# A gated mix of windowed attention and a GEGLU block: q weights and chunk 0's rows loaded another way, a few evictions and the last product changed

## The chip, the core and the metric

The kernel runs on one core of a Trainium2 chip. The core has TensorE (PE, matrix products; weight loads are listed as PEld), VectorE (DVE), ScalarE (ACT), GpSimd (POOL), SyncE (SP, which issues most DMAs), and 16 DMA engines. The metric is device time in microseconds (us) from start to end of one execution; a time of a kernel is the median of several executions. The profile is that of one execution.

## The reference

The input x has 2048 rows of 1024 columns, in bf16. Two blocks are applied to it and mixed row by row:

```python
g = sigmoid((x * gate_w).sum(-1, keepdims=True))
# block A: 32 heads of 32 columns; a row sees itself and 7 rows before it, 2 apart
q, k, v = split(x @ wqkv)                     # wqkv: 1024 x 3072
logits = q . k[pos - 2*w] / sqrt(32)          # w = 0..7, masked where pos - 2*w < 0
a = (softmax(logits) weighted sum of v[pos - 2*w]) @ wo
# block B: gate and up 1024 x 3584, down 3584 x 1024
b = (gelu(x @ w_gate) * (x @ w_up)) @ w_down
out = g * a + (1 - g) * b
```

## The kernel before, in words

**Tiling.** The rows form four chunks of 512, taken in two pairs (a pair is a "sup"). Each large product is done on 2 x 2 blocks with seven products in place of eight (Strassen-Winograd), so sums of weight blocks and of input blocks are needed. TensorE works on 128x128 weight tiles and 512 columns at a time; an accumulator is one of eight PSUM banks. Weights pass through `ring`, 20 slots of 256 KB. The columns of x (or of the weights' rows) come in eight tiles, kt = 0..7, halves of four.

**Stages.** For pair 0: q (`first_pair`), k, v projections (`qkv_pair`), then gate/up (`ffn`, 28 column tiles), then `down` for chunk 0. For pair 1: down and projections in the order q, v, k, and so on; `down(3)` is last, with seven products m for each of two row groups g. The attention of a chunk, with scores (L937, L943) and weighted sums (L1084 to L1102), is VectorE's work beside TensorE's products.

**What sets the order.** A planner, `Weave`, runs while the program is built. Each stream of work is a generator of operations with an estimated cost and dependencies. At every step the planner emits the head of the stream with the smallest start time plus bias. A stream's bias is dropped when the operation's `due` time is nearer than `AHEAD`. What it emits on one engine stays in that order on the chip. `main()` alone holds TensorE's operations, so their order is that of the text; the planner mixes VectorE's and the DMA issues.

**The start.** Chunk 0's rows, first half of their columns, come by two DMAs (L312): rows 0 to 255 from SyncE, 256 to 511 from ScalarE. `turn_rows` (L541 on) turns them on TensorE, four 128x128 transposes for each of four row tiles j; VectorE and ScalarE empty the four banks in turn (L561, L559), into `xs[0]`. The first product needs all four. The gate's weights ride along (L555, L564). The second half of the columns comes turned, by a DMA transpose in `early_x(0)` (L357), and so does chunk 1, in `early_x(1)`. The queue of SyncE (`loads`, L424) holds: the q weights of tiles 0 and 1 in one DMA of 512 KB, of 2 and 3 (L428), chunk 0's transpose, tiles 4 and 5, tiles 6 and 7, chunk 1's two transposes, then eight k tiles of 256 KB (L352), v (L434), and from L387 on the down weights that are prepared for later ("prep").

**The first product.** In `first_pair` with c = 0, four accumulators A[t] take tiles 0 and 1, one tile after the other, then 2 and 3 (L592). Each A[t] is then copied to a second bank, Bk[t] ("seed": ScalarE L604, VectorE L602 for odd t), because products go on in both. Tiles 4 to 7 follow, and ScalarE empties A[t] to q (L625). Then come, all under L772: for each t "product 5" of T1 and the sum `wqf` form 0, into Dk[t] (copied to m5, L637), with `gate(0)` and `gate(1)` (L874) before the first two of them; "product 6" of T2 and form 1 into Bk[t] (copied to u2, L648); then products of T3, B22 and T4, whose results are added on VectorE at L657 and L667.

**Sums.** `x_forms` makes T1 = b12 - b11 (L516), T2 (L518), T3 (L520, which waits for gate 1), T4 (L521) from chunk 0 (b11, b21) and chunk 1 (b12, b22). `qkv_forms` makes four sums for every two weight tiles (L709); one instruction covers both tiles through an access pattern with the distance of the two ring slots as its stride. `wforms` (L496) and `preps` (L470 to L475) do the same for gate/up and down weights.

**Gate.** `gate(c)` sums x * gate_w over columns on TensorE; VectorE turns the bank (L880), and the bank is free after that.

**Later projections.** In `qkv_pair`, L837 adds a bank and m5 for the product with T3, into k or v; the last product on that bank, with T4, waits for this addition.

**The end.** In `down_rest`, product m = 6 of group 1 is the last: 18 matmuls of 512 columns (L1305), one ScalarE eviction that scales (L1346), one store of 128 KB (L1338).

Of the kernel before, what the change touches and what calls it, by code (L numbers as in the profile page):

```python
# [8 lines left out]
ACT = mybir.ActivationFunctionType  # L9
# [34 lines left out]
class Weave:  # L44
# [7 lines left out]
    AHEAD = 11.75  # L52
# [102 lines left out]
def kernel(  # L155
# [68 lines left out]
    DUE = (77.1, 303.05)  # L224
# [86 lines left out]
    def load_rows(q, j, hf):  # L311
        q.dma_start(out=hrow[:, XR + j:XR + j + 2, hf * KH * P:(hf + 1) * KH * P],  # L312
                    in_=x[j * P:(j + 2) * P, hf * KH * P:(hf + 1) * KH * P].rearrange("(j p) n -> p j n", p=P))

    load_rows(nc.sync, 0, 0)
    load_rows(nc.scalar, 2, 0)
# [38 lines left out]
    def early_x(c):  # L355
        for hf in range(2) if c else (1,):
            o = Op("SP", (KH * P * SC * 2, 2.1), lambda hf=hf: nc.sync.dma_start_transpose(  # L357
                out=xq(c, hf), in_=x[c * SC:(c + 1) * SC, hf * KH * P:(hf + 1) * KH * P]), tail=1.2)
            yield o
            for k in range(KH):  # L360
                w.done[("x", 1, KH * hf + k) if c else ("pt", k, 1)] = o
# [11 lines left out]
    def load_prep(i0):  # L373
# [14 lines left out]
        return Op("SP", (4 * n * P * NW * 2, 2.0 * n), fn, [("preps", i0 - 2 * NSTG)] if i0 >= 2 * NSTG else [("qkv", 1, 0, t) for t in range(NT)] if si == 2 else [("gcol",)] if si == 1 else [],  # L388
# [35 lines left out]
    def loads():  # L424
        for kt in range(0, KT, 2):
            if kt == KH:
                yield from early_x(0)
            o = Op("SP", (2 * P * D * 2, 0.7), lambda kt=kt: nc.sync.dma_start(  # L428
                out=qbuf[:, kt:kt + 2], in_=qkv_src(0, kt, 2)), key=("wqkv", 0, 0, kt))
            yield o  # L430
            w.done["wqkv", 0, 0, kt + 1] = o
        yield from early_x(1)
# [30 lines left out]
    def preps():  # L463
        for i0 in range(0, NPREP, 2):
# [5 lines left out]
            f0 = dve(t, lambda: V(out=b11, in0=b12, in1=b11, op=ALU.subtract), due=DUE[0] + 3.05 * i0, deps=[("prep", i0), ], lag=1.0)  # L470
            yield f0
            yield dve(t, lambda: V(out=b12, in0=b22, in1=b12, op=ALU.subtract), due=DUE[0] + 3.05 * i0)
            f1 = dve(t, lambda: V(out=b22, in0=b22, in1=b11, op=ALU.subtract), [f0], due=DUE[0] + 3.05 * i0)
            yield f1
            last = dve(t, lambda: V(out=b21, in0=b21, in1=b22, op=ALU.subtract), [f1], due=DUE[0] + 3.05 * i0)  # L475
# [12 lines left out]
    def wforms():  # L488
        t = tt(GR)
        for b in range(NBLK):  # L490
            ops = []
            for f, x_, y_, op in ((0, "U21", "A22", ALU.add), (2, "A11", "U21", ALU.subtract), (1, 0, "A11", ALU.subtract),
                                  (3, "A12", 1, ALU.subtract)):
                def go(f=f, x_=x_, y_=y_, op=op, b=b):
# [4 lines left out]
                        due=DUE[0] + 12.1 * b)  # L499
# [9 lines left out]
    def x_forms():  # L509
        t = tt(KH * SC)  # L510
        for sup in range(NSUP):
# [4 lines left out]
            t1 = dve(t, lambda b12=b12, b11=b11: V(out=tf[:, 0], in0=b12, in1=b11, op=ALU.subtract), dx[0:KH] + free, lag=0.5, key=("xf", sup, 1), bias=-1.0)  # L516
            yield t1
# [25 lines left out]
    def turn_rows():  # L543
        for j in range(NST):
            i, free = bank_take()
            pt = banks[i][:].bitcast(BF16)[:, 0:KH * P].rearrange("p (k s) -> p k s", k=KH)

            def go(pt=pt, j=j):
                for kk in range(KH):
                    nc.tensor.transpose(out=pt[:, kk, :], in_=xrow(j, kk, 1), identity=ident)  # L550
            o = Op("PE", 0.24, go, [free] if free else [], tail=0.17)
            yield o
            if j == NST - 1:
                gt = banks[i][:].bitcast(BF16)[:, KH * P:KH * P + KT]
                og = Op("PE", 0.1, lambda: nc.tensor.transpose(out=gt, in_=grow, identity=ident[0:KT, 0:KT]), [], tail=0.17)  # L555
                yield og
            dst = xs[0][:, 0:KH, j * P:(j + 1) * P]
            if j % 2:
                e = act(0.58, lambda pt=pt, dst=dst: nc.scalar.copy(out=dst, in_=pt), [o], key=("pt", j, 0))  # L559
            else:  # L560
                e = dve(0.42, lambda pt=pt, dst=dst: nc.vector.tensor_copy(out=dst, in_=pt), [o], key=("pt", j, 0))  # L561
            yield e
            if j == NST - 1:
# [4 lines left out]
    def first_pair(c, prod, dst, ev, B11, B21, T1, T2, T3, B22, T4):  # L568
# [17 lines left out]
        def mm(t, kts):  # L586
            d = [("wqkv", c, 0, kt) for kt in kts] + [("x", ca, kt) for kt in kts if ca]                 + [("pt", j, kts[0] // KH) for j in range(NST) if not ca]
# [19 lines left out]

        if not c:
            for t in ts:
                A[t], fr[t] = bank_take(dirty=True)  # L610
            for kt in range(2):
                for t in ts:
                    yield mm(t, [kt])
        for t in ts:
# [3 lines left out]
            yield from seed(t)  # L618
        if not c:
            for t in ts:  # L620
                yield mm(t, [KH, KH + 1])
# [6 lines left out]
        for t in ts:  # L628
            if not c and t < 2:
                yield from gate(t)  # L630
            Dk[t], free = bank_take(dirty=t > 1)
            o = prod(Dk[t], 0, 0, T1, t, True, [free])
            yield o

            def cp(t=t):
                m5[t] = hold(t, 0, "m5")
                nc.scalar.copy(out=m5[t], in_=as_(t, banks[Dk[t]][:]))  # L637
            ev["m5", t] = act(0.48, cp, [o])
            yield ev["m5", t]
        for k in range(2):  # L640
            ring_give(("wqf", c, 0, 0, k), o)
        for t in ts:
            o = prod(Bk[t], 0, 1, T2, t, False, [ev["seed", t]])
            yield o

# [4 lines left out]
            yield ev["u2", t]  # L650
# [806 lines left out]
```

## Time and profile before

| what | value |
|---|---|
| median of three executions | 722.49 us (722.13 to 722.61) |
| profiled execution, span from first to last instruction | 720.13 us |
| TensorE busy | 710.1 us |
| granted TensorE clock, mean | 1.000 |
| DMA moved | 176.84 MB |
| VectorE busy, 0 to 36 us | 25.73 us |
| VectorE busy, 340 to 372 us, idle waits of over 0.5 us | 2.21, 0.52, 1.54, 2.75 us |
| chunk 0's attention, last operation | 251.53 us, 0.43 long |

How to read it. A row of a timeline has the start, the length, engine, line, operation, output<-input, shape and count; in brackets stands how long the engine was idle before it and what it waited for. A row of the waits has who waited, for whom, the total, the count and the longest. A group's mean duration of a matmul (379 ns) is its latency; matmuls overlap, and start every 0.216 us. A row of the stretches has the stretch, then each engine's busy time with its count in brackets (TensorE twice, products and weight loads, then VectorE, ScalarE, GpSimd), the clock, the share of the DMA engines and GB/s.

### The profile page before, as it was taken

To read this page: it belongs to the slowest core of one execution; us is meant where nothing else is said; L and a number is where in the kernel's file an instruction comes from. 1 tells how busy PE (TensorE), PEld (TensorE's weight loads), DVE (VectorE), ACT (ScalarE), POOL (GpSimd) and SP (SyncE) were. 2 spreads that over 40 slices of the span, in tenths; PEclk is the share of its full clock that TensorE was granted. 3 is DMA by queue.
4 is the path that set the end of the run, shared out by engine and by line. 5 is a ranking of instruction groups with operands and counts; after the bars stand their busy time and mean duration, and the time that the engine had idled before them with its cause. 6 is when DMAs were issued, how large, how long until landed. Compare 5 with 4: busy or idle time off the path is not lost.

```text
span 720.1 us, 9892 instructions
## 1 busy us (share of the span) xinstructions
PE 710.1 (99%) x3337; PEld 342.7 (48%) x3337; DVE 609.8 (85%) x862; ACT 323.8 (45%) x547; POOL 73.8 (10%) x130
## 2 busy tenths in 40 slices
PE   7999999999999999999999999999999999999997
PEld 3556544444444444456554444444444444444443
DVE  4989999999998999799789988799999997849300
ACT  3354585555585522153465323258556655310110
POOL 0020333343121100100000000100000000001000
PEclk9999999999999999999999999999999999999999
DMA  9953899996797799943378899996647656999992
GB/s 263 363 192 97 248 295 311 362 317 225 179 249 230 238 253 330 336 174 117 88 214 272 277 299 352 311 310 186 185 137 194 172 165 161 322 294 376 297 338 93
DMA packets 184179, 176.84 MB, mean 246 GB/s; under 512 B 58304, under 2 KB 140224, under 8 KB 184000
## 3 DMA queue, kind: packets, MB, share of 16 engines
q1 hardware_dynamic: 174512, 145.53, 68.6%
q0 software_dynamic: 9328, 30.42, 11.6%
q8 instruction: 26, 0.43, 0.2%
q10 hardware_dynamic: 288, 0.26, 0.1%
q14 instruction: 25, 0.20, 0.1%
HBM read 132.12 MB, written 31.46 MB: 227 GB/s over the span
## 4 chain that ended last, share of the span: by engine, by line
PE 96%; DVE 1%; SPq 1%; DMA 1%; issue 0%; ACT 0%; DVEq 0%
PE ps L1136 47%; PE ps L1305 30%; PE ps L772 18%; PE ps L592 1%; SPq L357 1%; DMA hT<-in_A_wqkv_dram 1%; DVE ring L709 0%; SPq L428 0%; DVE lend L837 0%; DVE tf L518 0%; DVE zt L880 0%; PE ps L874 0%; ACT ost L1346 0%; DVE hT L709 0%; PE ps L898 0%
## 5 line engine op out<-in xcount | busy, mean ns | idle before, releaser
L1136 PEld LDWEIGHTS <-ring 128*128 128x128 bf16 x1568 | 153.2, 98 | 185.1 <-issue 0.5
L1136 PE MATMUL ps<-lend,ring 128*128 128x512 bf16 x896 | 212.7, 379 | 0.0
L1136 PE MATMUL ps<-tf,ring 128*128 128x512 bf16 x672 | 164.3, 379 | 0.0
L1305 PE MATMUL ps<-ring,hT 128*128 128x512 bf16 x708 | 160.7, 379 | 0.0
L1305 PEld LDWEIGHTS <-hT 128*128 128x128 bf16 x708 | 69.1, 98 | 83.8 <-DVE ost L1380 0.4
L1084 DVE TENSOR_TENSOR xbuf<-xbuf,lend 128x2048 bf16<-128x2048 bf16 x64 | 77.5, 1217 | 16.6 <-DMA xbuf<-xbuf 16.5
L772 PEld LDWEIGHTS <-ring 128*128 128x128 bf16 x512 | 65.0, 127 | 49.6 <-issue 3.6
L937 DVE TENSOR_TENSOR xbuf<-qo,lend 128x2048 bf16<-128x2048 bf16 x64 | 77.0, 1218 | 2.3 <-ACT lend L830 2.3
L943 DVE TENSOR_TENSOR xbuf<-xbuf 128x2048 bf16<-128x2048 bf16 x56 | 68.2, 1218 | 0.2
L772 PE MATMUL ps<-tf,ring 128*128 128x512 bf16 x256 | 58.4, 380 | 3.2 <-DVE lend L837 1.4
L772 PE MATMUL ps<-lend,ring 128*128 128x512 bf16 x256 | 57.9, 379 | 0.0
L1346 ACT ACTIVATE ost<-ps,omg 128x512 bf16<-128x512 f32 x16 | 11.0, 687 | 101.3 <-PE ps L1305 89.7
L1168 ACT COPY ps<-ps 128x512 f32<-128x512 f32 x56 | 32.1, 573 | 51.8 <-PE ps L1136 51.6
L1212 ACT ACTIVATE gl<-ps 128x512 bf16<-128x512 f32 x56 | 33.5, 598 | 46.5 <-PE ps L1136 46.3
L1305 PE MATMUL ps<-ring,qo 128*128 128x512 bf16 x192 | 49.3, 380 | 0.0
L1338 POOL DMA_DIRECT2D out_dram<-ost x24 | 13.0, 541 | 336.6 <-ACT ost L1346 248.3
L1185 DVE TENSOR_TENSOR hT<-hT,gl 128x1024 bf16<-128x1024 bf16 x56 | 38.3, 685 | 8.6 <-ACT hT L1178 8.5
L505 POOL DMA_DIRECT2D fforms<-ring x56 | 30.8, 551 | 144.2 <-DVE ring L496 138.1
L1224 DVE TENSOR_TENSOR u<-ps,u 128x512 f32<-128x512 f32 x56 | 38.3, 685 | 2.7 <-PE ps L1136 2.3
L1228 ACT ACTIVATE gl<-u 128x512 bf16<-128x512 f32 x56 | 35.4, 633 | 11.3 <-DVE u L1224 10.7
L1220 ACT COPY u<-ps 128x512 f32<-128x512 f32 x56 | 32.8, 586 | 14.3 <-PE ps L1136 14.3
L1094 DVE TENSOR_TENSOR xbuf<-xbuf 128x2048 bf16<-128x2048 bf16 x32 | 38.9, 1217 | 0.1
(120 smaller groups left out, 668.8 us busy)
## 6 DMA issues: line engine op xcount, KB each, us to landing
ring<-dforms SPq DMA_DIRECT2D x112, 256.0 KB, 5.0
ring<-in_B_w_down_dram SPq DMA_DIRECT2D x84, 256.0 KB, 5.4
ring<-in_B_w_gate_dram SPq DMA_DIRECT2D x56, 256.0 KB, 5.4
fforms<-ring POOLq DMA_DIRECT2D x56, 256.0 KB, 5.2
ring<-fforms SPq DMA_DIRECT2D x56, 256.0 KB, 4.1
ring<-in_B_w_up_dram SPq DMA_DIRECT2D x42, 256.0 KB, 4.8
ring<-in_A_wqkv_dram SPq DMA_DIRECT2D x32, 256.0 KB, 4.5
ring<-oforms SPq DMA_DIRECT2D x32, 256.0 KB, 5.6
```

Source lines behind the costliest of these rows:

```text
L772: nc.tensor.matmul(banks[bk][:], lhsT=lhsT, rhs=rhs[:, kt, :], start=(start and kt == 0), stop=(kt == KH - 1), skip_group_check=True)
L937: V(out=w3(box[t]), in0=q_b, in1=k_w, op=ALU.mult)
L943: V(out=w3(box[0]), in0=w3(box[0]), in1=w3(box[t]), op=ALU.add)
L1084: return dve(tt(n), taking(("p", t), lambda: V(out=w3(box["p", t]), in0=w3(box["ab"]), in1=v_w, op=ALU.mult)), [("qkv", c, 2, t), abo] + ( ...
L1094: V(out=p0.rearrange("p (u n) -> p u n", u=2), in0=lo, in1=hi, op=ALU.add)
L1136: nc.tensor.matmul(banks[bk][:], lhsT=wv[:, k, fl * P:(fl + 1) * P], rhs=rhs[:, k, :], start=(start and k == 0), stop=(k == KH - 1), skip_ ...
L1185: yield dve(tt(2 * SC), lambda hv=hv, gv=gv: nc.vector.tensor_tensor(out=hv, in0=hv, in1=gv, op=ALU.mult), [e, ev[f, "g1"], ev[f, "g2"]], ...
L1212: nc.scalar.activation(out=gl[f][:, r1 * SC:(r1 + 1) * SC], in_=banks[A[f]][:], func=ACT.Gelu_apprx_tanh)
L1220: nc.scalar.copy(out=u2[f][:], in_=banks[Bk[f]][:])
L1224: e = dve(tt(SC, True), lambda f=f: nc.vector.tensor_tensor(out=u2[f][:], in0=banks[Dk[f]][:], in1=u2[f][:], op=ALU.add), [o, ev[f, "u2"]])
L1228: ev[f, "g2"] = act(0.54, lambda f=f: nc.scalar.activation(out=gl[f][:, r2 * SC:(r2 + 1) * SC], in_=u2[f][:], func=ACT.Gelu_apprx_tanh), [ ...
L1305: nc.tensor.matmul(banks[bk][:], lhsT=l, rhs=wv[:, i, :], start=(start and k == 0), stop=(q == last and i == 1), skip_group_check=True)
```

## The change

1. `loads` and `early_x`: q weights are loaded in eight DMAs of 256 KB. The second half of chunk 0's rows comes as rows, by one plain DMA of 512 KB between tiles 3 and 4; the DMA transpose of chunk 0 is gone.
2. `turn_rows(hf, kks)` turns one column block of all four row tiles at a time, for both halves (32 transposes in place of 16). Its place is inside `first_pair`: blocks 0 to 2, products of tile 0, block 3, products of tile 1, products of tiles 2 and 3, four blocks of the second half, then tiles 4 to 7. VectorE empties blocks 0 and 2 and the whole second half, ScalarE 1 and 3.
3. A[t] after tile 3 is kept in SBUF by ScalarE (`late`), and the four seeds are made from there by ScalarE after A[t] is emptied. The first prepared load (si = 0) waits for the seeds, since it writes the same memory.
4. The order after tile 7: gate 0; product 5 of t = 0 and 1, first on tiles 0 and 1, then on 2 and 3; gate 1; product 5 of t = 2, product 6 of t = 0, product 5 of t = 3, product 6 of the others. T1 is made in two halves. Gate 1's bank is copied to SBUF by ScalarE, and VectorE turns the copy.
5. `qkv_forms`: where the two tiles do not lie next to each other, a sum is made with one instruction per tile. Form 2 of q waits for T1. Due times: second projection 302.59 + 13.63 per weight + 2.54 per form (before 303.05, 23.0, 2.5); gate/up sums 80.01 + 11.51 per block (before 77.1, 12.1); preparations 80.01 + 2.82 per step (before 77.1, 3.05); `AHEAD` 12.35 (before 11.75). Four streams get other biases.
6. The last product of `down(3)` is done in two halves of 256 columns. ScalarE copies the upper half of the bank to another bank beforehand; each half has its own eviction and its own store of 64 KB.

The core of the diff (of parts 1 to 6):

```diff
-        for kt in range(0, KT, 2):
+        for kt in range(KT):
             if kt == KH:
-                yield from early_x(0)
-            o = Op("SP", (2 * P * D * 2, 0.7), lambda kt=kt: nc.sync.dma_start(
-                out=qbuf[:, kt:kt + 2], in_=qkv_src(0, kt, 2)), key=("wqkv", 0, 0, kt))
+                yield Op("SP", (KH * P * SC * 2, 0.6), lambda: load_rows(nc.sync, 0, NST, 1), key=("xr", 1))
+            yield Op("SP", (P * D * 2, 0.5), lambda kt=kt: nc.sync.dma_start(
+                out=qbuf[:, kt:kt + 1], in_=qkv_src(0, kt, 1)), key=("wqkv", 0, 0, kt))
...
-    def turn_rows():
-        for j in range(NST):
+    def turn_rows(hf, kks=range(KH)):
+        for kk in kks:
...
+                for j in range(NST):
+                    nc.tensor.transpose(out=pt[:, j * P:(j + 1) * P], in_=xrow(j, KH * hf + kk, 1), identity=ident)
...
+            for t in ts:
+                A[t], fr[t] = bank_take()
+            yield from turn_rows(0, range(3))
+            for t in ts:
+                yield mm(t, [0])
+            yield from turn_rows(0, [3])
+            for t in ts:
+                yield mm(t, [1])
...
+                def keep(t=t):
+                    late[t] = hrow[:, FT - 4 + t, :].bitcast(F32)
+                    nc.scalar.copy(out=late[t], in_=banks[A[t]][:])
...
+            for t in ts:
+                Bk[t], free = bank_take(True)
+                ev["seed", t] = act(0.5, lambda t=t: nc.scalar.copy(out=banks[Bk[t]][:], in_=late[t]), [ev["kept", t]] + ([free] if free else []))
+                yield ev["seed", t]
+            for kts in ((0, 1), (2, 3)):
+                for t in ts[:2]:
+                    yield from first5(t, kts)
+            yield from gate(1)
+            yield from first5(2)
+            yield from second6(0)
+            yield from first5(3)
+            for t in ts[1:]:
+                yield from second6(t)
...
-                    return _win_ap(w0[:, KH * hi:KH * hi + 1], [[w1.offset - w0.offset, 2], [NT, P], [1, KH]])
+                    step = w1.offset - w0.offset
+                    if step == D:
+                        return [_win_ap(w0[:, KH * hi:KH * hi + 1], [[D, 2], [NT, P], [1, KH]])]
+                    return [_win_ap(z[:, KH * hi:KH * hi + 1], [[NT, P], [1, KH]]) for z in (w0, w1)]
...
-                                 bias=(0.1, -0.6)[which == 0] if which < 2 and not sup else None,
-                                 due=DUE[1] + 23.0 * QVK.index(which) + 2.5 * f if sup else 0.0)
+                                 bias=(0.05, -0.75)[which == 0] if which < 2 and not sup else None,
+                                 due=DUE[1] + 13.63 * QVK.index(which) + 2.54 * f if sup else 0.0)
...
+            za = work.tile([P, 2 * SC], BF16, tag="gl", bufs=3, name="za")[:].bitcast(F32)
+            e = act(0.48, lambda: nc.scalar.copy(out=za, in_=banks[i][:]), [o])
...
+                elif last and g == 1:
+                    hw = NW // 2
+                    o = yield from prod(Bk[g], m, g, False, [ev[g, "x"]], (0, hw))
+                    e = act(0.4, lambda g=g, om2=om2, box=box: nc.scalar.activation(
+                        out=ost_tile(box)[:, 0:hw], in_=banks[Bk[g]][:, 0:hw], func=ACT.Copy, scale=om2), [o])
+                    yield from evac(e, j2, 0, box, 0, hw)
+                    bank_give(Bk[g], e)
+                    o = yield from prod(hi, m, g, False, [ev["hi"]], (hw, NW))
```

## The prediction

> **What bounds the kernel now.** I read the page first: busy shares, then the chain that ended last.
>
> ```profile
> PE 710.1 (99%) x3337; PEld 342.7 (48%) x3337; DVE 609.8 (85%) x862; ACT 323.8 (45%) x547; POOL 73.8 (10%) x130
> ...
> PE 96%; DVE 1%; SPq 1%; DMA 1%; issue 0%; ACT 0%; DVEq 0%
> ```
>
> TensorE is busy for 710.1 of 720.1 us, and the chain runs on it for 96%. A matmul of 512 columns starts every 0.216 us (20 take from 20.76 to 25.08), and the change leaves their number alone. So only TensorE's roughly 10 us of idle time can move. Where does it lie? Its waits, and its timeline at the start:
>
> ```profile
> PE ps L592 <- DMA hT<-in_A_wqkv_dram: 1.5, 1, 1.5
> PE ps L772 <- DVE lend L837: 1.4, 2, 0.9
> PE ps L772 <- DVE tf L516: 1.0, 1, 1.0
> PE ps L322 <- DVE xbuf L320: 0.9, 1, 0.9
> PE ps L772 <- DVE zt L880: 0.8, 1, 0.8
> PE ps L592 <- ACT lend L559: 0.7, 1, 0.7
> ```
>
> ```profile
> 4.31 1.07 PE L550 MATMUL ps<-hT 128*128 128x128 bf16 x16
> 5.32 0.17 PE L555 MATMUL ps<-hT,xbuf 8*128 8x8 bf16 x1
> 6.16 3.61 PE L592 MATMUL ps<-lend,hT 128*128 128x512 bf16 x16 [0.67 <-ACT lend L559]
> 11.28 3.67 PE L592 MATMUL ps<-lend,hT 128*128 128x512 bf16 x16 [1.50 <-DMA hT<-in_A_wqkv_dram]
> 14.89 0.61 PE L874 MATMUL ps<-lend,gcol 128*32 128x512 bf16 x8
> 16.52 1.05 PE L772 MATMUL ps<-tf,ring 128*128 128x512 bf16 x4 [1.02 <-DVE tf L516]
> 17.50 0.61 PE L874 MATMUL ps<-lend,gcol 128*32 128x512 bf16 x8
> 18.05 1.92 PE L772 MATMUL ps<-tf,ring 128*128 128x512 bf16 x8
> 20.76 4.48 PE L772 MATMUL ps<-tf,ring 128*128 128x512 bf16 x20 [0.80 <-DVE zt L880]
> ```
>
> Five waits end before 20.8 us: 0.9 that the change does not touch, and 0.67 + 1.50 + 1.02 + 0.80 = 4.0 us of queries' stage. From 20.76 to 716.4 TensorE waits only twice, 1.4 us together, both for L837. After 716.4 come the last eviction and store, 3.7 us to the span's end.
>
> **The start, step by step.** Why does tile 4 of the q weights land only at 11.28? In the DMA view its pair is issued at 7.28, because SyncE spends 2.27 to 7.24 on the DMA transpose of chunk 0's second half. Landings before: weight pairs at 5.95 and 7.4, that transpose 9.3, pairs 11.3 and 12.7, chunk 1's halves 14.8 and 16.8. From these rows 512 KB of plain load take 1.45 us, 512 KB of transpose 2.0.
>
> After the change the queue holds four q tiles, the second half of the rows as a plain load, four q tiles, then chunk 1's transposes. Chained from 7.4: rows 8.85, tiles 5 and 7 at 10.3 and 11.75, chunk 1 at 13.85 and 15.9. So chunk 1 comes 0.9 us earlier.
>
> TensorE after, from 4.31, with 16 transposes at 1.07 us, 0.216 a matmul, 0.42 a VectorE eviction, 0.585 one on ScalarE. The first column block needs one transpose group and one eviction, where now all four rows' evictions are awaited; the row halves of the two queues land at 4.25 and 4.55, so products begin near 5.35 instead of 6.16. Four for tile 0 end at 6.2, the fourth group and the gate row at 6.5, tile 1 at 7.4, tiles 2 and 3 at 9.15. The 16 added transposes end at 10.2 (rows 8.85, so no wait), tiles 4 and 5 at 11.95, tiles 6 and 7 at 13.7, gate 0 at 14.3. Here the cover is thin: four VectorE evictions, 0.44 apart, end at 11.35 before tile 7 needs the last at 12.2; a VectorE sum slipped in front would take 0.6 of that 0.85. ScalarE copies four kept products (0.57 each, done 10.35), evicts four, and seeds four banks by 16.85; product 6 needs the first at 18.2.
>
> Then VectorE decides, as now. Half of T1 needs chunk 1's first half: 13.85 + 0.65 = 14.5. Gate 0's transpose follows (0.64), then the second half of T1 to 15.85, then T2 (needs 15.9) to about 17.2. Product 5 for two tiles, first halves: 14.55 to 15.4. Second halves: 15.9 to 16.75. Gate 1: to 17.35. Product 5 of tile 2 to 18.2, 6 of tile 0 to 19.1, 5 of tile 3 to 19.95, three more of 6 to 22.55. The same products now end at 25.08: **minus 2.5 us**. What is late next is T1's second half (0.5). Gate 1's bank is copied by ScalarE (0.58) before VectorE turns it; nobody on TensorE waits for that bank, so nothing is priced. Bounds: without any wait after the first eviction the work would end at 21.8, minus 3.3; if chunk 1 lands no earlier than now, all behind it is 0.95 later, minus 1.6.
>
> A rule against tile-by-tile loads: the Trainium skill, DMA: Bandwidth & Descriptors, section Bandwidth, says to batch transfers to 1 MiB for three quarters of peak. Taken literally it would make q weights of 256 KB slower than the pairs, and the gain smaller. This trace's 256 KB K tiles land eight in about 6 us, some 0.35 MB/us, as fast as the pairs, so the row decides.
>
> **The middle.** All queued behind the start moves 2.5 us earlier: K tiles, V, block weights. VectorE must keep up, being full in mid-run:
>
> ```profile
> 108.00:144.00 36.00, 36.00 (x169) 16.30 (x168) 35.61 (x51) 19.89 (x36) 11.96 (x19) 1.00 1.05 336
> 144.00:180.00 36.00, 36.00 (x168) 16.30 (x167) 35.90 (x55) 19.88 (x37) 14.17 (x22) 1.00 0.80 271
> 180.00:216.00 36.00, 36.00 (x168) 16.32 (x167) 35.62 (x55) 24.56 (x41) 7.03 (x13) 1.00 0.93 214
> ```
>
> The fourth number is VectorE's busy time in 36 us. The cover: chunk 0's attention ends at 251.96 and TensorE reads its second half at 259.4, 7.5 us later; the blocks' sums are done some 12 us before their products. TensorE 2.5 us earlier leaves 5. The first load of the down weights to be prepared now waits for the seeds, done at 16.85, while SyncE reaches it at 20: free.
>
> Sums per tile: a 128x1024 sum takes 0.60 from start to start, a 128x512 one 0.35. So each split costs 0.10, at most 32 of them 3.2 us, 2.4 of it in the second projection (309 to 383 us). There VectorE idles 7.0 us between 340 and 372, so I price it at nothing.
>
> The moved due times reorder VectorE. In the second projection the sums of V and K come due 10 and 19 us earlier. Now this happens:
>
> ```profile
> 339.10 2.35 DVE L937 TENSOR_TENSOR xbuf<-qo,lend 128x2048 bf16<-128x2048 bf16 x2
> 341.37 2.48 DVE L943 TENSOR_TENSOR xbuf<-xbuf 128x2048 bf16<-128x2048 bf16 x2
> 343.76 1.28 DVE L837 TENSOR_TENSOR lend<-ps,m5q 128x512 bf16<-128x512 f32 x2
> ```
>
> Long attention operations stand before the short addition that TensorE's last product needs. Bounds: both waits go (minus 1.4), or one 1.2 us operation stands before each of four groups of V and K (plus 4.9, less the 1.4). I take **minus 0.5**: the sums come forward and clear VectorE around 351 to 361, but which operation then stands ahead is not in this trace.
>
> **The end.**
>
> ```profile
> 716.44 0.69 ACT L1346 ACTIVATE ost<-ps,omg 128x512 bf16<-128x512 f32 x1 [3.20 <-PE ps L1305]
> ```
>
> The last product is 18 matmuls, 3.88 us; halved by columns it is 36 of 256. The transposes (128 columns) start 0.057 apart, the others 0.216; between them 256 columns give 0.110, 36 give 3.96: plus 0.08. The first half's eviction and store lie beside the second half. A ScalarE eviction costs 0.172 for 8 columns and 0.585 for 512, 0.82 ns each, so half saves 0.21. The store now lands 1.7 after issue; half the bytes, perhaps 0.05. Sum **minus 0.2**, bounds minus 0.4 and plus 0.2. The extra ScalarE copy of the upper half comes 8 us before its use: free.
>
> A rule against halves: the Trainium skill, TensorE: Matmul & The Clock Gate, sections LDWEIGHTS and The mechanism, gives a weight load of 128 columns 128/1.2 = 107 ns, and says that loads overlap running matmuls only in another row group. Exposed for all 36, that would add some 3.9 us (an estimate from that page) and spoil the change. Here loads of 98 ns sit inside a 216 ns rhythm and even inside 57 ns between transposes, so I go by the rows.
>
> **Sum.** The profiled execution spans 720.13 us, the median is 722.49; the 2.36 around the span I leave unchanged. 722.49 - 2.5 - 0.5 - 0.2 = **719.3 us**.
>
> **Rivals.** *The start gains less.* Chunk 1's transposes land as late as now, or an eviction stands behind a sum, and VectorE's mid-run waits take another part: minus 1.6 at the start and nothing else is 720.9; with 1 us given back, 721.9. For it: VectorE, not DMA, ends three of the start's waits. Against: no transpose stands before the last q tiles any more, and later there are 5 us of cover. *Nothing is left,* 722.5: attention 0 loses all its 7.5 us of cover. Against: needs three times the shift. *Slower.* In the second projection each of the four groups of V and K waits 1.2 us for one long operation ahead of L837: plus 4.9 - 1.4 - 2.7 = plus 0.8, and with the split sums' 2.4 us not hidden, plus 3.2: **725.7**. It decides once those waits together exceed 1.4 (there now) + 2.7 (gained elsewhere) + 1.4 (measurable) = 5.5 us. For it: this is the one place where TensorE already waits in mid-run. Against: 7 us of VectorE idle time there.
>
> **Chances.** Forecast with its bounds (717.2 to 720.9) 0.68, below 717.2 0.04, a smaller or no gain (720.9 to 723.9) 0.17, slower 0.11. A measurement of this kernel can tell 0.2%, 1.4 us, from no change. Faster by more (under 721.0) takes the first two and 0.01 of the third: 0.73; within: 0.16; slower: 0.11. The low end is both bounds of the start and the middle, 722.49 - 3.3 - 1.4 - 0.4 = 717.4, a little lower for rounding; the high end, 722.4, leaves out the slower case and some of the third.
>
> **What would show it.** Right: products from about 5.4 us, tile 4 landed near 10, queries' sixth product done near 22.5 us, the last eviction near 0.48 us, waits for L837 of at most 1.4. Wrong: product 5 starting after 15.5, evictions at L561 spread by sums, 256-column matmuls more than 0.12 apart, or new TensorE waits between 25 and 716 us, first of all on L837.

## The result, and the profile after

The changed kernel takes **720.64 us** (median of 7 executions, 720.01 to 722.01), the kernel before 722.49 in the same comparison (7 executions, 722.13 to 723.71). The ratio is 0.9971, with an interval of 0.9961 to 0.998: faster by some 0.3%. The profiled executions span 718.5 and 720.13 us, 1.6 apart. The forecast was 719.3: the gain came, at 1.85 us in place of 3.2.

The page of the kernel after, busy shares:

```profile
PE 708.3 (99%) x3305; PEld 345.7 (48%) x3371; DVE 610.9 (85%) x888; ACT 326.9 (45%) x556; POOL 73.9 (10%) x130
```

TensorE is as full as it was, so its few waits say more. Those of after (who waited, for whom, total, count, longest), but for the 0.9 at the very start that the change does not touch:

```profile
PE ps L826 <- DVE lend L891: 1.8, 1, 1.8
PE ps L826 <- DVE tf L515: 0.4, 1, 0.4
PE ps L826 <- ACT u2q L667: 0.3, 1, 0.3
```

L826 is the former L772, and L891 the former L837. Of the 4.0 us that the queries' stage waited, 0.4 is left, and a new 0.3 (for a ScalarE copy, L667) has come. Two waits of 1.4 together for L837 have become one of 1.8 for L891. TensorE's timeline at the start:

```profile
4.39 1.57 PE L552 MATMUL ps<-hT 128*128 128x128 bf16 x12
5.75 1.16 PE L595 MATMUL ps<-lend,hT 128*128 128x512 bf16 x4
...
16.41 1.02 PE L826 MATMUL ps<-tf,ring 128*128 128x512 bf16 x4 [0.41 <-DVE tf L515]
...
23.12 1.03 PE L826 MATMUL ps<-lend,hT 128*128 128x512 bf16 x4
24.47 2.75 PE L826 MATMUL ps<-lend,hT 128*128 128x512 bf16 x12 [0.32 <-ACT u2q L667]
```

The row at 23.12 is the first product of T3, which began at 25.08 before: 1.96 earlier. Four matmuls later comes the new wait; when the twelve behind it are through, at 27.06 (28.53 before), 1.47 is left. Where it went from there, read from the same products in both timelines:

| place on TensorE | before | after | difference |
|---|---|---|---|
| first matmul with T3 | 25.08 | 23.12 | -1.96 |
| 16 matmuls later | 28.53 | 27.06 | -1.47 |
| down, chunk 0 | 250.80 | 249.78 | -1.02 |
| behind the place of the first wait for L837 | 344.50 | 342.38 | -2.12 |
| behind the second (L837, L891) | 369.27 | 368.51 | -0.76 |
| last product | 712.35 | 711.30 | -1.05 |
| end of the span | 720.13 | 718.5 | -1.6 |

So the start gives 2.0, its new wait takes 0.5 back, the middle as a whole gives back another 0.4, and the end gives 0.6. Most of these have their own experiments below. The row at L891, and its counterpart before:

```profile
368.51 1.89 PE L826 MATMUL ps<-tf,ring 128*128 128x512 bf16 x8 [1.79 <-DVE lend L891]
```

```profile
369.27 1.89 PE L772 MATMUL ps<-tf,ring 128*128 128x512 bf16 x8 [0.44 <-DVE lend L837]
```

### The profile page after: what moved, and what is told of

The parts are those of the page before. It is cut to its first block, busy times and chain, and to the rows that moved or that the text cites. A ratio compares the mean times of both kernels' runs of the same rounds, so it can differ in the third digit from the quotient of the medians.

```text
span 718.5 us, 9947 instructions
## 1 busy us (share of the span) xinstructions
PE 708.3 (99%) x3305; PEld 345.7 (48%) x3371; DVE 610.9 (85%) x888; ACT 326.9 (45%) x556; POOL 73.9 (10%) x130
## 4 chain that ended last, share of the span: by engine, by line
PE 84%; issue 10%; DVE 3%; DMA 2%; POOL 1%; ACT 0%; DVEq 0%; POOLq 0%; ACTq 0%
PE ps L1198 45%; PE ps L1367 26%; PE ps L826 10%; DMA parked<-hT 1%; PE ps L595 1%; DMA ring<-dforms 1%; DMA ring<-in_B_w_down_dram 1%; PE ps L322 1%; POOL out_dram L1400 0%; PE ps L552 0%; DVE ring L494 0%; DVE u L1286 0%; DVE xbuf L1091 0%; DVE hT L1265 0%; DVE tf L519 0%
## 5 line engine op out<-in xcount | busy, mean ns | idle before, releaser
L1367 PE MATMUL ps<-ring,hT 128*128 128x512 bf16 (+1 forms) x704 | 159.6, 375 | 0.9
L1367 PEld LDWEIGHTS <-hT 128*128 128x128 bf16 x722 | 70.6, 98 | 82.6 <-DVE xbuf L1005 0.4
L826 PEld LDWEIGHTS <-ring 128*128 128x128 bf16 x512 | 64.7, 127 | 48.5 <-issue 3.1
L826 PE MATMUL ps<-tf,ring 128*128 128x512 bf16 x250 | 58.1, 379 | 2.5 <-DVE lend L891 1.8
L826 PE MATMUL ps<-lend,ring 128*128 128x512 bf16 x251 | 57.6, 379 | 0.3
L1367 PE MATMUL ps<-ring,qo 128*128 128x512 bf16 (+1 forms) x193 | 49.1, 375 | 0.2
```

Source lines behind the costliest of these rows:

```text
L826: nc.tensor.matmul(banks[bk][:], lhsT=lhsT, rhs=rhs[:, kt, :], start=(start and kt == 0), stop=(kt == KH - 1), skip_group_check=True)
L1367: nc.tensor.matmul(banks[bk][:, o0:o0 + cols[1] - cols[0]], lhsT=l, rhs=wv[:, i, cols[0]:cols[1]], start=(start and k == 0), stop=(q == la ...
```

## The experiments

A planner writes the order of the instructions, and a small edit moves others far from it: a ratio belongs to the edit with its new order, so each wait is also read in its place. Ratios are to the kernel before, run in the same comparison, with their intervals.

**The last product alone.** The kernel before, with part 6 only (functions `down` and `down_rest` of after):

```diff
+                elif last and g == 1:
+                    hw = NW // 2
...
```

> The kernel before with the last product in halves and nothing else. From the two traces, the end is worth 0.6 us: the half eviction takes 0.47 in place of 0.69, and 2.6 us in place of 3.0 pass from its end to the span's end, less 0.06 of matmuls. Theory: 721.9 us (minus 0.6). Rival, as forecast: only the eviction gets shorter and the store does not, minus 0.2, so 722.3. A second rival, exposed weight loads under 256 columns, would show matmuls more than 0.12 us apart and a time above 722.5.

Measured: 722.16, ratio 0.9995 (0.9982 to 1.0007): in the total nothing can be told, neither the 0.6 expected nor the rival's 0.2. In the rows it can. ScalarE's last eviction in after:

```profile
715.44 0.47 ACT L1466 ACTIVATE ost<-ps,omg 128x256 bf16<-128x256 f32 x1 [1.49 <-PE ps L1367]
```

Here it lies at 716.63, and takes 0.47 too, for 0.69 before. From the start of the last product (711.30 in after, 712.50 here) to the end of this eviction it takes 4.61 and 4.60 us; before, 712.35 to 716.44 + 0.69, 4.78. That is 0.17 less, where the forecast's own terms gave plus 0.08 and minus 0.21, so minus 0.13. From there to the span's end it is 2.6 in after, 2.9 in this kernel, 3.0 before: a store of half the bytes saves 0.1 here and 0.4 in after. From the start of the last product to the span's end it is 7.8 in two executions of the kernel before, and 7.1 to 7.5 in all twelve kept traces with the halves (7.2 or less in ten of them). So the end gives 0.3 to 0.7. The span, 720.0, hides it because this execution's start was slow, which TensorE's timeline shows:

```profile
4.32 1.91 PE L550 MATMUL ps<-hT 128*128 128x128 bf16 x16
```

The start of this kernel is that of before, where the same 16 transposes took 1.07; here 1.91, and T3 begins at 25.70, not 25.08.

**The gate's bank read by VectorE again.** Gate 1 without ScalarE's copy:

```diff
-        if c == 1:
+        if c == -1:
             za = work.tile([P, 2 * SC], BF16, tag="gl", bufs=3, name="za")[:].bitcast(F32)
```

> The changed kernel with gate 1's bank read by VectorE directly, at once, as before. Theory: TensorE's 0.48 us wait for ScalarE's copy u2 comes from the buffer that gate 1's turned copy shares with u2, because VectorE turns it only at 22.3 us. With the turn early, that wait goes and the T3 product of the second tile starts where the first ends: 0.3 to 0.5 us less up to 30 us of the span, if no other wait takes its place. Rival: ScalarE's copy had freed VectorE for T1 and T2, and the direct read puts 0.7 us in front of them, so product 5 or 6 starts up to 0.7 later and the stage ends no earlier or later.

Measured: 727.43, ratio 1.0064 (1.0043 to 1.0085). The direct cost is there, a wait of TensorE for the bank, "PE ps L826 <- DVE zt L942: 1.0", and T3 starts at 24.13 in place of 23.12. So at T3 the copy is worth 1.0. The wait for L667 is gone here, as expected, and the products behind the 16 of T3 start at 27.58, in after at 27.06: less its own new wait, the copy is worth 0.5. The rest of the loss is not the gate's own: in this order VectorE stands idle for 5.06 us before a weight sum at 131.56 that waits for a DMA, with the addition for TensorE's bank (L1265) behind it. TensorE waits 2.90, and then, in its timeline:

```profile
128.12 1.89 PE L1198 MATMUL ps<-lend,ring 128*128 128x512 bf16 x8
132.91 3.57 PE L1198 MATMUL ps<-tf,ring 128*128 128x512 bf16 x8 [2.90 <-DVE hT L1265]
```

Eight matmuls take 1.89 ahead of the wait and 3.57 behind it. The next eight start at 136.27, and the ones after those at 139.31: 16 need 6.40 for 16 x 0.216 = 3.46. The wait costs its 2.9 and another 2.9 behind it, while the clock column reads 0.50 to 0.77 (1.00 again from 140). A second wait, 2.47 for ScalarE (L1256) at 477.77, leaves the clock alone.

**The first sums of down(1) behind the second projection.** The last additions of the projection, into k, wait on VectorE behind sums of the next stage. This edit makes those sums (S1, from L1328) depend on the projection's last product:

```diff
-                home = [("pr", c - 1, 6, 1)] + ([("parked", 2)] if c == 1 else []) if c % 2 else ...
+                home = [("pr", c - 1, 6, 1)] + ([("parked", 2), ("qkv", 2, 1, KH + 1)] if c == 1 else []) if c % 2 else ...
```

> The changed kernel where the first sums of the down stage of chunk 1 stand behind the two additions into k on VectorE, in place of ahead of them. Theory: the 1.79 us that TensorE waits at 368 us is no lack of VectorE time; these sums wait for the parked copy of v to land (365.6 us) and hold back the additions queued behind them. With the order turned round, that wait goes: minus 1.7 us, 718.9. Rival: VectorE is short of time there, and another operation or the bank freed by the addition behind the sums holds TensorE as long: minus 0.5 or less, 720.1 or more.

Measured: 719.53, ratio 0.9953 (0.9937 to 0.9968), between the 718.9 expected and the rival's 720.1; the interval just overlaps that of after (0.9961 to 0.998), so the gain in the total is likely, not certain. The wait at 368 is gone. VectorE's timeline there, before, after and in this kernel:

```profile
366.40 2.22 DVE L1266 TENSOR_TENSOR hT<-hT 128x1792 bf16<-128x1792 bf16 x2 [2.75 <-DMA parked<-hT]
368.54 1.28 DVE L837 TENSOR_TENSOR lend<-ps,m5q 128x512 bf16<-128x512 f32 x2
```

```profile
365.63 2.22 DVE L1328 TENSOR_TENSOR hT<-hT 128x1792 bf16<-128x1792 bf16 x2 [3.81 <-DMA parked<-hT]
367.77 1.28 DVE L891 TENSOR_TENSOR lend<-ps,m5q 128x512 bf16<-128x512 f32 x2
```

```profile
367.22 0.69 DVE L891 TENSOR_TENSOR lend<-ps,m5q 128x512 bf16<-128x512 f32 x1 [2.41 <-PE ps L826]
...
368.69 1.08 DVE L1328 TENSOR_TENSOR hT<-hT 128x1792 bf16<-128x1792 bf16 x1
```

In the first two VectorE is not busy but idle, 2.75 and 3.81 us, until the store of V to DRAM ("parked", 1 MB) has landed and its memory may be written by the sum; the addition that TensorE waits for stands behind. In the third the addition comes first and waits only for TensorE's own product. The profiled execution has other waits in exchange (0.9 for a q tile at the start, 1.46 for ScalarE at 142.44), so its span, 719.4, is not short; the median is. (The wait for ScalarE near 140 comes in after itself too, in one of two executions, as shown further on, so it is not put down to this edit.)

**Chunk 0's second half by DMA transpose again.** 16 transposes on TensorE less, a DMA transpose between tiles 3 and 4:

```diff
-                yield Op("SP", (KH * P * SC * 2, 0.6), lambda: load_rows(nc.sync, 0, NST, 1), key=("xr", 1))
+                o = Op("SP", (KH * P * SC * 2, 2.1), lambda: nc.sync.dma_start_transpose(
+                    out=xq(0, 1), in_=x[0:SC, KH * P:2 * KH * P]), tail=1.2)
...
-            yield from turn_rows(1)
```

> The changed kernel with chunk 0's second half turned by DMA again, and no transposes of it on TensorE; q tiles still one by one. Theory: that DMA transpose ahead of q tiles 4 to 7 holds SyncE and the queue, tile 4 lands near 11 us as in the kernel before, products of tile 4 start near 11.3 in place of 10.8, chunk 1 lands 0.6 to 0.9 later, and the q stage's T3 products start 0.5 to 1.5 us later than 23.1. Rival: VectorE's sums and the gate's turn set the stage, not the landings; then the T3 products start within 0.3 of 23.1, and saving four evictions on VectorE even helps.

Measured: 722.97, ratio 1.0009 (0.9998 to 1.002). The wait for tile 4 is back, in TensorE's timeline:

```profile
11.35 3.93 PE L599 MATMUL ps<-lend,hT 128*128 128x512 bf16 x16 [1.31 <-DMA hT<-in_A_wqkv_dram]
```

T3 starts at 24.22, 1.1 later than in after, and nothing is left of the gain in the total: 722.97 is 2.3 above after. The 1.1 at the start is the part that the rows explain. The other half was not followed; part of it can lie in the planner's new order. Without the transposes on TensorE, then, no gain of the rest of the change can be told.

**One instruction per sum.** The sums of part 5 with one access pattern over both tiles, whatever their distance:

```diff
-                    if step == D:
-                        return [_win_ap(w0[:, KH * hi:KH * hi + 1], [[D, 2], [NT, P], [1, KH]])]
+                    if True:
+                        return [_win_ap(w0[:, KH * hi:KH * hi + 1], [[step, 2], [NT, P], [1, KH]])]
```

> The changed kernel, same order on every engine, but every weight sum of two tiles is one VectorE instruction again, with the slots' distance as its stride. Theory: the split sums cost VectorE about 0.1 us each where it has time to spare, so the total stays within 0.3 us of the changed kernel. Rival A: VectorE is short in the second projection, the time falls by 0.5 to 2 us. Rival B: the wide access pattern also covers slots that lie between, makes sums wait for loads that they do not need, and the time rises by over 0.5.

Measured: 719.7, ratio 0.9957 (0.994 to 0.9973); the intervals overlap that of after, so the total says little. The profiled span is the same 718.5. The wait of 1.79 at 368 is gone, a wait of 1.10 for ScalarE has come at 140.63, and before 343.98, where after has none, TensorE waits for L891 again, in the row of its waits:

```profile
PE ps L826 <- DVE lend L891: 0.2, 1, 0.2
```

This holds in every kept trace: a wait at 343 to 346 stands in all six with one instruction per sum (0.25 to 1.49), in none of the eight with split sums. So the split goes with the loss of the first wait, and with the growth of the second. The traces say more than the totals here. The store's issue on GpSimd's queue and the first loads for the next stage on SyncE's, in after and then in this kernel (start, time to issue):

```profile
357.27 0.85 POOL L781 DMA_DIRECT2D parked<-hT  x1 [23.31 <-ACT hT L912]
```

```profile
354.23 0.38 SPq L400 DMA_DIRECT2D ring<-in_B_w_gate_dram  x1
...
357.23 0.38 SPq L400 DMA_DIRECT2D ring<-in_B_w_up_dram  x1
```

```profile
358.87 0.85 POOL L781 DMA_DIRECT2D parked<-hT  x1 [23.72 <-ACT hT L912]
```

```profile
355.83 0.38 SPq L400 DMA_DIRECT2D ring<-in_B_w_gate_dram  x1
359.44 0.33 SPq L400 DMA_DIRECT2D ring<-fforms  x1
...
```

With one instruction per tile, all six loads of 256 KB are out by the time the store is issued. With one per sum SyncE first waits for a sum ("SPq L400 <- DVE ring L761: 3.2", 9.0 before), and five of the six come with the store or behind it, the last at 362.60. The store then takes 8.3 us to land in after and 6.5 here. It is issued 1.6 later here, since TensorE is later (by 1.65 at the wait's place), and still lands 0.2 earlier. This divides all 14 traces without an exception: 7.5 to 8.3 us in the eight with split sums, 6.0 to 6.9 in the six without. That the earlier loads delay the store is the reading that fits; the loads alone were not moved, so it is not shown.

**The old due times and biases,** with the rest of the change kept. The biases put back are those of five streams (the list of the change says four), and of the q sums:

```diff
-    AHEAD = 12.35
+    AHEAD = 11.75
-    DUE = (80.01, 302.59)
+    DUE = (77.1, 303.05)
...
```

> The changed kernel with the due times, AHEAD and stream biases of before. Theory: the start is as in the changed kernel within 0.5 us; in the second projection TensorE waits for the additions into v again (0.9 us near 343), and at 368 it waits less, since it arrives later against the same landing; in all within 0.7 us of the changed kernel. Rival: the new due times carry a gain of their own in mid-run, and without them the time rises by 1.5 us or more.

Measured: 729.35, ratio 1.0088 (1.007 to 1.0106), slower than either. The last weighted sums of chunk 1's attention (L1164) run to 423.26; in after they end at 403.43, before at 400.67. TensorE waits for them, in its timeline, and the stretches behind that wait (TensorE busy, weight loads, VectorE, ScalarE, GpSimd, then clock, DMA share, GB/s) show the price:

```profile
417.08 1.03 PE L1367 MATMUL ps<-ring,qo 128*128 128x512 bf16 x2 [3.48 <-DVE qo L1164]
```

```profile
416.00:418.00 2.00, 0.92 (x3) 0.38 (x4) 2.00 (x3) 0.00 (x0) 0.00 (x0) 0.54 0.79 287
418.00:420.00 2.00, 2.00 (x6) 0.66 (x5) 2.00 (x4) 0.68 (x2) 0.00 (x0) 0.50 0.01 2
```

The clock column reads 0.54 and 0.50 here, 0.50 and 0.75 in the next two stretches, and 1.00 from 424: 20 matmuls take 7.23, to 424.31, for 4.32. It read much the same behind the wait in the gate's kernel. The wait for L891 is 1.71 and none comes at 343, as in after: so the new due times neither removed the wait at 343 nor made the one at 368. What they and the new biases do, together, is to keep chunk 1's attention ahead of TensorE. The old ones did so in the kernel before (to 400.67); beside the rest of the change they no longer do. Which single value matters was not tried.

**q weights in pairs of 512 KB again:**

```diff
-            yield Op("SP", (P * D * 2, 0.5), lambda kt=kt: nc.sync.dma_start(
-                out=qbuf[:, kt:kt + 1], in_=qkv_src(0, kt, 1)), key=("wqkv", 0, 0, kt))
+            if kt % 2 == 0:
+                o = Op("SP", (2 * P * D * 2, 0.7), lambda kt=kt: nc.sync.dma_start(
+                    out=qbuf[:, kt:kt + 2], in_=qkv_src(0, kt, 2)), key=("wqkv", 0, 0, kt))
...
```

> The changed kernel with q weights loaded in four DMAs of two tiles. Theory: tile 0 then lands with tile 1, near 6.0 in place of 5.4, TensorE's first product starts 0.2 to 0.6 later, and since TensorE sets the pace up to gate 0, the q stage's T3 products come 0.2 to 0.6 later. Rival: chunk 1's landing and VectorE set the pace, nothing moves by more than 0.2.

Measured: 721.57, ratio 0.9983 (0.9972 to 0.9993). The first product starts at 5.89 (5.75 in after), T3 at 23.12, as in after. The rival's case came: nothing at the start moves by more than 0.2. The interval overlaps that of after, and the waits at 140 (1.1, which after has too in one of two executions) and 368 (1.5, in after 1.8) name no loss. No gain of loading tile by tile, by itself, is shown.

**A buffer of its own for gate 1's turned copy,** so that it does not wait for, and hold, one of the two "u2" buffers:

```diff
-        zt = work.tile([P, SC], F32, tag="m5" if c > 1 else "u2", bufs=2, name="zt")
+        if c == 1:
+            zt = lend[5][:].rearrange("p t s -> p (t s)")[:, 0:2 * SC].bitcast(F32)
+        else:
+            zt = work.tile([P, SC], F32, tag="m5" if c > 1 else "u2", bufs=2, name="zt")[:]
```

> The changed kernel, its order kept, with gate 1's turned copy in a buffer of its own, so that u2 needs not wait for it. Theory: TensorE's wait for ScalarE's u2 copy (0.32 shown, 0.48 by the start times) goes, and the products after T3 start 0.3 to 0.5 us earlier; the total gains at most that, and may gain nothing, since the wait near 368 for the landing of the parked v takes back what comes before it. Rival: ScalarE is itself late there, and the wait stays.

Measured: 720.67, ratio 0.9965 (0.9952 to 0.9978). The new wait of the start is gone, 16 matmuls run on in TensorE's timeline, and the next start at 26.36:

```profile
22.90 3.62 PE L826 MATMUL ps<-lend,hT 128*128 128x512 bf16 x16
```

Of the 0.70 gained here (27.06 in after), 0.22 is T3's own earlier start. The wait for L891 comes with 1.39, but TensorE is past it at 367.69, 0.82 ahead of after: the store, issued at 356.86 in place of 357.27, moved too. At the last product 0.36 is left (710.94), at the span's end 0.4. The intervals of the totals are too wide to tell so little.

**All three:** own buffer, one instruction per sum, sums of down(1) behind the projection.

> Three edits on the changed kernel together: gate 1's own buffer, one instruction per weight sum, and the first sums of chunk 1's down stage behind the additions into k. Theory: with nothing left at 368 to take the gains back they add up, minus 0.5 at the start and minus 1.2 to 1.8 at 368, about 718.5 us, a clear gain over the changed kernel (720.6). Rival: VectorE's queue, held by another late landing in the gate/up stage, takes the gain back, 719.5 or more.

Measured: **719.16**, ratio 0.9944 (0.9931 to 0.9957), span 717.8. This interval lies wholly below after's: the three together beat both kernels, though less than the 718.5 expected. Which of the three carries it is not separated: one instruction per sum alone had already taken the wait at 368 away. TensorE's longest wait, but for the untouched 0.9 at the very start (the others over 0.2 us are 0.6 in two for T1, L515, and 0.3 for L710):

```profile
343.76 1.89 PE L826 MATMUL ps<-tf,ring 128*128 128x512 bf16 x8 [0.74 <-DVE lend L891]
```

It stands behind long attention operations: the wait that the prediction shows for the kernel before, here again with one instruction per sum.

**And T1's second half ahead of gate 0's transpose,** added to the last:

```diff
-            e = dve(0.63, lambda: nc.vector.transpose(out=zt, in_=banks[i][:]), [o], bias=-2.0 if c < 2 else None)
+            e = dve(0.63, lambda: nc.vector.transpose(out=zt, in_=banks[i][:]), [o], bias=0.0 if c < 2 else None)
```

> As the run with the three edits, and T1's second half goes ahead of gate 0's turn on VectorE. Theory: TensorE's 0.4 us wait for T1's second half goes, chunk 1's second half (landing near 16.2) is next, so 0.1 to 0.4 us less at the T3 products and in the total. Rival: the planner's order after it changes, and the difference in mid-run is larger than that, in either direction.

Measured: 720.91, ratio 0.9968 (0.9956 to 0.9981): worse than the three alone, with intervals that just touch. Product 5 no longer waits between its halves, but TensorE waits 0.9 for the gate's bank (za, L939) and 0.4 for zt, and T3 starts at 24.29. Of the two orders at 15 us, the one that after has is the better.

**After and before once more,** one execution each:

> The changed kernel once more, unaltered, for one more profile. Theory: in its first profile TensorE still ran at half rhythm during the twelve transposes (1.57 us, first product at 5.75), and when that half rhythm ends differs between executions of one kernel. A second profile may show the transposes in 1.04 to 1.6 us, and first products, gate 0 and T3 products shifted by the same 0 to 0.6 us: if the transposes take under 1.2 us, T3 starts at 22.5 to 22.8. Rival: the late first product belongs to the changed kernel's order, and the second profile shows 5.7 and 23.1 again whatever the transposes take.

> The kernel before once more, unaltered, for one more profile. Theory: its sixteen transposes took 1.07 us in the first profile and 1.91 in the run with only the last product halved, same start; so the T3 products start anywhere from 25.0 to 25.8. Rival: they start at 25.1 again, and the 25.7 was that run's own.

Measured: 721.21 (span 719.4) and 723.07 (span 721.3). After: 12 transposes in 1.49, T3 at 22.91, again a wait for L667 (0.43) and for L891 (1.66), and one of 0.74 for ScalarE at 140.48. Before: 16 transposes in 1.07, T3 at 25.85, since the q pair landed later (wait 2.08). So the two new waits of after recur, the wait near 140 comes and goes without any edit, and the start of one kernel varies by some tenths to over half a microsecond from execution to execution.

## Why the prediction was right, and where it was not

**The start: right in mechanism and size.** Forecast minus 2.5, with T3 at 22.55; measured 23.12. The difference is at the very beginning: 12 transposes took 1.57 in place of some 0.8, and products began at 5.75, not 5.35. In other executions with the same start they take 1.03 to 1.06, and products begin at 5.32 to 5.35, as forecast. T3 then starts at 22.58 (one sum), 22.90 (own buffer) or 23.23 (all three). Over the seven kept traces with this start T3 lies at 22.58 to 23.32, and once at 24.17, where a q tile was late; over the three with the start of before at 25.08, 25.70 and 25.85. The middle values, 23.12 and 25.70, are 2.6 apart; the closest pair of the usual ones is 1.8 apart. So the forecast's 2.5 is met as well as single executions can tell. The wait named as next, for T1's second half, is there with 0.41 (0.5 forecast). That 1.1 of it comes from the DMA transpose, as said, is shown by the kernel that has it back: with it came the wait for tile 4 and T3 at 24.22. Another 1.0 is the gate's copy (T3 at 24.13 without it). Turning by column blocks, the earlier first eviction, was not tried alone.

**Gate 1's copy: the step that failed here.** "Nobody on TensorE waits for that bank, so nothing is priced" was true of the bank and missed the copy's destination. VectorE and ScalarE in after:

```profile
22.31 0.70 DVE L939 STREAM_TRANSPOSE zt<-za 128x512 f32<-128x512 f32 x1
...
23.58 0.17 DVE L946 COPY zq<-zt 128x16 f32<-128x16 f32 x1
```

```profile
23.83 0.59 ACT L667 COPY u2q<-ps 128x512 f32<-128x512 f32 x1 [2.52 <-DVE zq L946]
```

The turned copy shares two buffers with u2, VectorE comes to it only at 22.31, and ScalarE waits 2.52 for the buffer to empty product 6; TensorE's next product waits for that bank. It costs 0.5 by the starts (24.47 less 23.12 is 1.35, for four matmuls of 0.216), and a buffer of its own removes it.

**The middle: the wrong cause.** Forecast minus 0.5, measured plus 0.4. The prediction put both waits for L837 on long attention operations and moved due times. The first, at 343, does stand behind such operations, and it went; but it stays away with the old due times too, and comes back with one instruction per sum. So the term's first half came out with the split sums, which the prediction had priced at nothing, and not by the due times: that was luck. For the second wait, 0.44 before and 1.79 after, long operations are not the cause. VectorE idles there, behind a sum that waits for the store of V. The store was issued 2.1 earlier (357.27 against 359.39), as much as TensorE was ahead, but took 1.4 longer to land. Its issue before, and then its rows of the DMA view before and after (size, us from issue to landing):

```profile
359.39 0.85 POOL L727 DMA_DIRECT2D parked<-hT  x1 [24.41 <-ACT hT L858]
```

```profile
parked<-hT POOLq DMA_DIRECT2D x1, 1024.0 KB, 6.9
```

```profile
parked<-hT POOLq DMA_DIRECT2D x1, 1024.0 KB, 8.3
```

So it landed only 0.7 to 0.8 earlier, the wait grew by 1.35, and most of what had been gained by then was given back at this one place. The prediction had read "VectorE idles 7.0 us between 340 and 372" as room; 2.75 of it was this wait, with TensorE's addition queued behind. Making the sums stand back takes the wait away (719.53), which shows where it comes from; that its end is worth something in the total is clear of noise only together with the other two edits (719.16). Split sums, priced at nothing for VectorE's time, go with a changed order of the DMA issues instead; that these issues are what makes the store slow is argued, not shown. The 0.45 lost between 28 and 250 lies near 200 us, in two short waits (0.19 and 0.27); no experiment was made on it.

**The end: right sign, too small.** Forecast minus 0.2, measured minus 0.3 to 0.7. Product and eviction came out at minus 0.17, near the minus 0.13 worked out; the store, put at 0.05, gave 0.1 to 0.5. 36 matmuls of 256 columns start 0.109 apart, 3.94 us in all (forecast 3.96), with the weight loads inside. The estimate from the page on weight loads, plus 3.9, does not hold here. That the end gave more than forecast, and so covered part of the two misses before it, is luck.

**The rivals.** The one that came nearest is the smaller gain, 720.9, for the wrong reason: the start gave its full size, and the copy's buffer and a slower transfer took part of it back. The slower case did not come as it was put. The kernel with the old due times and biases shows that VectorE can fall behind, in attention and not in the second projection (6.7 above the kernel before), and that the new due times and biases of part 5 keep this away.

## What to carry to other kernels

An idle stretch of an in-order engine is not room: ask what it waits for, and what that the critical engine needs is queued behind it. A gain at the start survives only as far as every later wait moves with it. Here a transfer was issued 2.1 earlier but landed only 0.8 earlier, so follow a gain from landmark to landmark, and a transfer to its landing. A wait that is there in one execution of an unaltered kernel and not in the next says nothing of an edit. When a value gets a new copy, price the buffer that the copy goes into, not only the bank that it leaves.

## What the runs showed of the hardware

**Two waits of about 3 us cost some double.** Behind waits of 2.90 and 3.48 us (gate's kernel, old due times) the granted clock read 0.50 to 0.54 at first and was back at 1.00 some 7 us later; each cost about 2.9 us more than the wait itself (6.40 for 3.46, and 7.23 for 4.32). A wait of 2.47 us (gate's kernel) left the clock at 1.00. The Trainium skill, TensorE: Matmul & The Clock Gate, section What's actually happening, has the gate drop to half after an idle window of about 3.4 us; the 2.90 here was already enough.

**The first transposes run slowly for another length of time in each execution.** With the same program up to there, they took 1.03 to 1.57 for 12 and 1.07 to 1.91 for 16. In the slowest case each of the 16 lasted 0.311 us, in the quickest about 0.22. That moved the first product from 5.32 to 5.75 and from 6.12 to 7.02. T3 does not follow it alone: behind equally quick transposes it started at 22.58 and at 23.23. The clock column read 1.00 all the while, so no row here shows the clock as the cause. The same section of that page says that the window runs freely and that the start therefore varies from run to run, which agrees with the scatter.

**A 1 MB store's landing time went with what the other queue had sent just before it:** 6.0 to 6.9 us where one of the 256 KB loads had gone out ahead of it (six traces), 7.5 to 8.3 where six had (eight). No run moved the loads alone.
